# Turning the inverse transform's result by transposing DMAs within SBUF instead of on TensorE, for three of five channel groups

## The chip, the cores and the metric

The kernel runs on one core of one Trainium2 chip. The metric is the device time of one execution in microseconds (us), lower being better. The time before is the median of seven executions; a profile of one execution shows what each engine did in it.

## What is computed

The reference has two independent halves whose results are joined along the last axis. Half A is attention with a compressive memory, over four segments of 512 positions and 32 heads of 18 channels. Half B is a long convolution along the sequence, which the reference writes with Fourier transforms:

```python
# half A, for each segment s of 4 (L = 512, H = 32 heads, Dh = 18)
logits = einsum('bhqd,bhkd->bhqk', qs, ks) * scale + mask
a_dot  = einsum('bhqk,bhkd->bhqd', softmax(logits), vs)
a_mem  = einsum('bhld,bhde->bhle', phi(qs), M) / (einsum('bhld,bhd->bhl', phi(qs), z) + 1e-6)
o      = g * a_mem + (1 - g) * a_dot
M, z   = M + einsum('bhld,bhle->bhde', phi(ks), vs), z + sum(phi(ks))
a      = concat(o) @ wo                         # (2048, 576)
# half B (S = 2048 positions, D = 576 channels)
kv = shift4(k, shift_k) * v                     # a causal filter of 4 taps per channel
y  = irfft(rfft(pad(kv)) * rfft(pad(ssm_k)))[:S]
b  = q * (y + kv * ssm_D)
out = concatenate([a, b], axis=-1)              # (2048, 1152)
```

## The kernel before

All work is written down as some 1,360 pieces in a graph: each piece names the engines that may run it, what it reads and writes, and a priority. `schedule` deals the pieces to the five engines with a list scheduler that uses fixed durations, the priorities of the table `PRIO` (one integer for every piece, in the order in which pieces are created), the number of buffers of each kind (`SLOTS`) and the eight PSUM banks. It runs when the kernel is built; on the chip each engine then goes through its list in that order and waits on semaphores. So the table sets the order of everything, and a piece can be dealt to ACT or DVE, or to DVE or POOL, according to it. Almost all DMAs are issued from SP's queue, in list order; only the loads of `wq` and `wk` are issued from ACT.

Half A. For each segment, five transposing loads (L1032) bring x as `xT`; projections make queries and keys (`dn`), which go out to a scratch tensor in DRAM and come back per group of four heads as `pad` (L1073, three buffers). For each of the 32 head groups three score pieces on PE (L1293) are followed by exponentials on ACT (L1303, L1306), triangular masks on POOL (L1314) and the product with V on PE. The sums and results pass through DRAM scratch (`a_scratch`, `rs_scratch`) to be spread over partitions again as `cs`, `rs`, `rd` and `am`.

Half B. The channels are cut into five groups: four of 128 and one of 64. For each group:

- keys and values are loaded by transposing DMAs (L609, L612), filtered by matmuls with diagonal weights, multiplied and written to a scratch tensor; the filter `ssm_k` (kind h) and the product (kind x) are loaded as `xs`;
- `Dt`, a constant tensor made from `ssm_D`, is loaded once (L584) and added to the filter by `dadd` (L684) before its transform;
- two transform stages on PE (F1, F2) give spectra, which DVE and POOL multiply (`PQ`, L743 and L754);
- the inverse's first stage (`inv`) goes through PSUM and is copied to the tile `C` in four octants (`eC`). There is one buffer for `C`;
- **the turn**: `C` holds 128 partitions by 4096, which are 32 squares of 128x128 (16 in the last group). Eight at a time are transposed on PE against the identity into one PSUM bank (L802, the piece `ct`), and the bank is copied to a tile `CTp` of 128x1024 by ACT or DVE (the piece `ect`). There are three buffers for `CTp`;
- the inverse's last stage (`last`) multiplies the turned squares with the table `Psi`, DVE multiplies the result with q (L824, the piece `y`), and two DMAs store it (L831).

Groups 0 to 3 have four turns of eight squares each, group 4 has two: 18 turns in all.

The copies that the prediction names are those of helper `copy`: L365 on ACT, L367 on DVE. Matmuls go through `mm` (L359, and L361 for those placed in a part of the array). `zz` is a zeroed tile from which three DMAs (L985 and L992) fill the unused rows of the scratch tensor behind `pad`.

Of the kernel before, what the change touches and what calls it, by code (L numbers as in the profile page):

```python
# [12 lines left out]
ACT = mybir.ActivationFunctionType  # L13
# [5 lines left out]
P = 128  # L19
# [12 lines left out]
def c_act(n):  # L32
    return 0.06 + n * 0.00083
# [298 lines left out]
class Prog:  # L332
# [325 lines left out]
    def build_b(self):  # L658
        g, p = self.g, self.p
        for gi, (c0, Cg) in enumerate(GROUPS):  # L660
# [128 lines left out]
            for w in range(nc4 // 16):  # L789
                pl = Buf("ps2", "pslast")  # L790
                for v in range(2):
                    pt = Buf("ps1", "psct")
                    ct = Buf("CTp", "CTp")
                    vv = 2 * w + v
                    pr = tl + 2 * w + v

# [7 lines left out]
                    self.pe("ct%d.%d" % (gi, vv), 8 * 147, 8, tr, [Ct, self.ident], [pt], pr, al=[ct])  # L804
# [4 lines left out]
                    g.add("ect%d.%d" % (gi, vv), {"ACT": c_act(1024), "DVE": 0.075 + 1024 * 0.00052}, et, r=[pt], w=[ct], prio=pr)  # L809
# [671 lines left out]
    CV=[-35.266, 50.144, 61.906, 109.44, 129.026], flex=[-91.722, -31.756], lag_fin=193.527, pmode='d', qmode='f',  # L1481
)
# [17 lines left out]
-1149 -38 5 18 72 99 114 -74 -19 5 51 88 64 128 146 167 159 180 165 122 131 30 186 118 228 48 101 100 108 251 306 256  # L1500
263 352 380 245 253 21 331 182 192 229 -316 142 243 275 281 277 290 311 307 336 409 459 380 479 497 531 571 565 597
621 710 642 560 803 790 817 854 840 881 934 970 875 981 1058 1072 1085 1281 1268 1295 1346 1509 1296 1395 1491 1511
1525 1548 1538 1565 1582 109 63 10 89 -333 -29 95 64 60 224 310 27 229 284 281 119 208 60 236 249 29 54 253 109 83 255
-111 104 108 106 116 73 113 110 121 112 115 172 125 185 155 162 208 178 194 208 263 300 331 318 328 339 201 218 240
325 364 244 329 480 373 593 433 605 692 199 213 243 244 190 161 255 262 374 393 386 403 361 387 380 373 440 461 453
463 201 209 223 167 228 226 225 239 247 231 143 252 340 349 349 355 411 414 390 396 462 478 462 474 498 399 413 433
343 351 371 375 386 407 442 453 550 467 473 492 443 435 463 508 517 594 571 577 601 537 543 561 516 523 545 687 693
701 496 501 512 599 606 623 645 654 698 679 685 704 591 631 640 651 658 686 763 769 848 719 724 739 746 756 783 828
836 851 812 819 844 839 841 876 863 870 890 923 932 947 917 925 945 893 899 924 957 966 1044 764 804 922 1088 1114
1157 958 624 979 951 864 997 1237 939 1282 1198 1099 1251 1184 1155 1218 1331 1341 1350 1366 1321 1307 1322 1351 1469  # L1510
1462 1490 1525 1839 1832 1847 1860 341 352 376 486 498 560 575 593 631 656 671 723 708 743 735 751 819 869 882 890 608
696 757 856 927 871 819 965 1072 1174 1240 1355 1442 627 646 665 671 622 643 668 694 713 745 742 750 708 726 755 763
752 794 798 806 784 850 842 859 815 847 908 923 810 840 906 912 948 960 957 967 943 954 963 973 539 533 547 984 978
993 991 997 1006 972 964 981 1014 1028 1143 1178 1266 1245 1184 1253 1266 1295 1338 1354 1273 1321 1329 1359 1425 1376
695 699 770 778 836 838 930 938 1026 1030 1241 1255 1419 1068 1076 1094 1005 1012 1034 953 964 986 1105 1125 1148 1101
1107 1142 1163 1171 1182 1200 1210 1198 1183 1194 1218 1350 1357 1377 1133 1142 1164 1391 1408 1443 1237 1242 1269
1208 1214 1235 1292 1302 1339 1277 1339 1310 1326 1333 1352 1302 1309 1333 1367 1379 1386 1374 1383 1403 1398 1410
1430 1442 1456 1462 1428 1437 1457 1450 1461 1481 1475 1489 1509 1526 1537 1543 1534 1540 1562 1507 1513 1548 1576
1586 1591 1513 1544 1569 1630 1701 1741 1607 1258 1645 1654 1599 1838 1858 1904 1781 1852 1907 1892 1919 1871 1989
2004 1905 1864 1933 1946 2029 2021 2056 2053 2040 2046 2055 2077 2137 2143 2152 2164 2130 2123 2144 2157 1022 1029  # L1520
1049 1060 1075 1138 1114 1153 1180 1168 1185 1212 1187 1227 1378 1358 1401 1432 1413 1454 1167 1199 1280 1449 1517
1343 1539 1528 1696 1777 1829 1614 1915 1166 1177 1198 1203 1259 1291 1293 1298 1207 1216 1253 1258 1269 1312 1307
1321 1274 1287 1321 1335 1325 1348 1351 1360 1429 1466 1513 1524 1437 1469 1523 1537 1478 1488 1559 1572 1482 1498
1588 1598 1150 1157 1169 1621 1627 1636 1588 1613 1623 1602 1596 1611 1634 1652 1679 1734 1829 1834 1926 2006 2054
1944 2035 2046 2064 2108 2124 2057 2094 2099 1256 1265 1299 1306 1355 1371 1558 1562 1645 1650 1698 1713 2130 1560
1567 1586 1609 1616 1635 1584 1591 1609 1664 1679 1722 1693 1701 1722 1659 1666 1686 1736 1745 1752 1773 1779 1800
1719 1725 1743 1743 1750 1770 1817 1827 1839 1825 1832 1820 1800 1807 1796 1861 1870 1879 1905 1914 1907 1856 1863
1850 1881 1888 1877 1960 1970 1978 1932 1938 1923 1956 1962 1954 2004 2018 2024 2078 2087 2107 2016 2023 2011 2053
2061 2049 2115 2139 2146 2110 2116 2146 2155 2161 2181 2200 2210 2217 1934 2036 2072 2245 2267 2285 2100 1883 2135
2149 2107 2150 2195 2207 2352 2175 2395 2418 2302 2168 2340 2359 2316 2238 2365 2392 2471 2465 2479 2497 2496 2503  # L1530
2512 2521 2552 2558 2567 2581 2586 2592 2602 2621 1635 1663 1684 1700 1640 1805 1789 1817 1748 1777 1789 1868 1890
1927 1909 1921 1932 2082 2097 2108 1832 1805 1896 1947 2123 1959 2082 2312 2177 2380 2493 2435 2617 2046 2060 2066
2080 1861 1868 1873 1877 2105 2121 2159 2164 2012 2021 2063 2037 2134 2146 2162 2176 1760 1766 1775 2212 2220 2226
2247 2236 2254 2254 2261 2269 2188 2210 2229 2250 2304 2307 2427 2532 2538 2370 2389 2421 2258 2312 2325 2399 2434
2439 1618 1624 1618 1657 2376 2382 2410 2208 2215 2235 2182 2189 2224 2422 2432 2439 2243 2249 2269 2299 2309 2326
2357 2376 2383 2430 2437 2456 2352 2358 2417 2400 2409 2434 2478 2488 2501 2486 2492 2515 2454 2464 2502 2454 2464
2476 2510 2516 2537 2535 2542 2562 2599 2605 2627 2658 2668 2681 2570 2576 2603 2628 2634 2654 2672 2722 2693 2654
2661 2696 2833 2843 2932 2725 2730 2755 2877 2892 2919 2948 2961 2987 2974 2759 2768 2788 2696 2707 2727 2805 2815
2857 2899 2912 2861 2886 2567 2585 2611 2704 2724 2745 2640 2485 2685 2695 2656 2604 2691 2698 2769 2722 2812 2829
2779 2729 2816 2832 2970 2986 2978 2987 2995 3007 3085 3094 3076 3093 3098 3106 3068 3083 3046 3065 3087 3096 3025  # L1540
3039 3017 3038 3046 3050 250 346 388 470 365 381 382 406 362 373 511 610 620 619 631 590 599 604 609 417 425 668 692
686 699 713 897 911 428 431 698 849 708 858 871 943 954 432 440 935 1028 942 1035 1047 1091 1103 774 783 1036 1038
1042 1044 1063 1082 1093 92 186 1225 1233 1486 1230 1239 1480 1501 1260 1279 1648 1521 1530 1654 1667 1727 1746 515
606 816 830 779 793 908 918 785 804 779 1049 1049 1043 1048 1054 1060 1407 1408 1009 1016 1566 1679 1577 1687 1700
1945 1958 1456 1471 1711 1724 1716 1736 1749 1992 2003 1685 1692 1981 1987 1993 1994 1975 2065 2077 1886 1894 2150
2159 2165 2179 2196 2227 2236 1791 1798 2288 2294 2346 2294 2300 2333 2354 2316 2324 2381 2365 2369 2388 2394 2412
2418 773 869 1969 1977 1894 2010 1936 1945 1976 1983 1093 2278 2285 2283 2294 2177 2184 2272 2280 2001 2008 2308 2323
2313 2333 2344 2514 2526 2060 2069 2328 2340 2333 2348 2370 2412 2426 2267 2275 2438 2459 2445 2467 2480 2575 2594
2371 2375 2540 2559 2548 2566 2577 2603 2616 2457 2463 2632 2641 2685 2639 2648 2691 2702 2649 2657 2730 2720 2727
2736 2748 2765 2772 1457 1557 2490 2498 2445 2454 2614 2701 2393 2400 1982 2564 2572 2679 2688 2666 2674 2623 2630  # L1550
2644 2652 2701 2742 2713 2750 2761 2786 2797 2713 2720 2755 2768 2770 2781 2794 2819 2836 2750 2759 2795 2813 2802
2825 2834 2890 2906 2781 2788 2828 2847 2836 2862 2873 2900 2915 2845 2832 2926 2938 2948 2937 2956 2993 3001 2942
2965 2995 2954 2974 2999 3013 3033 3026 2290 2331 2800 2812 2840 2848 2626 2860 2872 2866 2875 2870 2883 2909 2914
2925 2925 2932 2961 2983 2884 2897 2921 2932 2936 2947 2957 3006 3022 1564 1557 2993 3040 3054 3041 3048 3060 3068
3082 3088
"""


def plan(prm=PRM, slots=SLOTS):
    pr = Prog(prm)  # L1560
    pr.build()
    if PRIO:
# [61 lines left out]
```

## Time and profile before

| | |
|---|---|
| median of 7 executions | 328.21 us (328.01 to 333.07) |
| the profiled execution | 330.75 us |
| its span in the profile | 329.0 us |
| mean granted TensorE clock | 0.964 of full speed |
| PE, DVE, ACT, POOL busy | 278.8, 254.0, 254.4, 154.8 us |
| DMA, SP's queue | 113,280 packets, 48.08 MB |

The span runs from the first to the last instruction on the core; the execution's own time is longer by what lies around it. PE is TensorE's matmuls, PEld its weight loads, DVE is VectorE, ACT is ScalarE, POOL is GpSimd, and SP is SyncE, whose row in a timeline (SPq) shows the time that its queue spends on issuing each DMA. A group's line ends with the idle time of the engine just before those instructions, and with what ended that idle time. The chain of work is followed back from the last instruction to what released it, step by step.

### The profile page before, as it was taken

The numbers are of one execution on the slowest core, as the hardware profiler recorded it, in microseconds if no ns is written. First come the engines' busy times: TensorE is split into PE (matmuls) and PEld (weight loads), VectorE is DVE, ScalarE is ACT, GpSimd is POOL, SyncE is SP. The second block draws the span as 40 slices with busy tenths as digits, with TensorE's granted clock in tenths as the row PEclk, the third lists the DMA queues.
The fourth block names the chain that finished last, engine by engine and source line by source line (L and its number), as shares of the span: only waits on it lengthen the run. The fifth ranks groups of instructions, "written<-read, shape, count | busy, mean of one in ns | idle before, by whom it ended". The sixth has DMA issues, their size and how long they took to land.

```text
span 329.0 us, 9734 instructions
## 1 busy us (share of the span) xinstructions
PE 278.8 (85%) x4073; PEld 190.6 (58%) x4083; DVE 254.0 (77%) x383; ACT 254.4 (77%) x251; POOL 154.8 (47%) x192
## 2 busy tenths in 40 slices
PE   1799779879898899898997998798987999886993
PEld 1656456455556665545565555555775576775882
DVE  6765666689797866867979558958899878998973
ACT  2465458798979889999977688879888889895940
POOL 8602032438546523855755237736738554325500
PEclk9999957999999999999999799989999999997998
DMA  8956898979998786499465795823343945143025
GB/s 183 304 91 203 164 175 204 146 222 196 154 183 182 178 140 187 156 262 210 141 147 116 141 251 191 175 95 116 103 122 91 189 143 133 59 89 64 4 57 114
DMA packets 114540, 50.03 MB, mean 152 GB/s; under 512 B 92206, under 2 KB 107328, under 8 KB 114496
## 3 DMA queue, kind: packets, MB, share of 16 engines
q1 hardware_dynamic: 113280, 48.08, 64.7%
q10 hardware_dynamic: 1216, 1.33, 1.6%
q8 instruction: 32, 0.52, 0.7%
q14 instruction: 12, 0.10, 0.1%
HBM read 25.31 MB, written 16.87 MB: 128 GB/s over the span
## 4 chain that ended last, share of the span: by engine, by line
PE 37%; ACT 21%; DVE 16%; DMA 12%; issue 7%; SPq 4%; POOL 1%; ACTq 0%; DVEq 0%; POOLq 0%
PE PS L359 24%; ACT P L1303 11%; PE PS L361 7%; DMA wq<-in_A_wq_dram 5%; PE PS L1293 4%; ACT P L1306 3%; DMA rs<-rs_scratch 3%; DVE PQ L743 2%; DMA Dt<-in_B_ssm_D_dram 2%; SPq L992 2%; DVE C L367 1%; DVE Hx L367 1%; DVE dn L367 1%; DMA qk_scratch<-dn 1%; ACT PQ L365 1%
## 5 line engine op out<-in xcount | busy, mean ns | idle before, releaser
L1314 POOL TENSOR_SCALAR_AFFINE_SELECT P<-P 128x512 bf16<-128x512 bf16 (+1 forms) x112 | 81.6, 741 | 107.7 <-ACT P L1303 70.8
L1303 ACT ACTIVATE P<-PS 128x2048 bf16<-128x2048 f32 x54 | 101.6, 1881 | 14.3 <-PE PS L1293 12.4
L1306 ACT ACTIVATE P<-PS 128x1024 bf16<-128x1024 f32 x52 | 50.6, 1031 | 6.3 <-PE PS L1293 6.3
L1293 PE MATMUL PS<-pad 25*128 25x384 bf16 (+3 forms) x512 | 35.1, 306 | 7.7 <-ACT P L1303 5.6
L359 PE MATMUL PS<-A,Ft 128*128 128x128 bf16 (+1 forms) x480 | 33.7, 220 | 7.6 <-DVE PQ L743 3.1
L359 PEld LDWEIGHTS <-Ft 128*128 128x128 bf16 x480 | 28.3, 101 | 13.0 <-issue 11.6
L361 PE MATMUL PS<-W,xs 128*64 128x128 bf16 x576 | 23.7, 235 | 8.3 <-DVE xs L684 3.6
L754 POOL TENSOR_TENSOR PQ<-PQ,Hx 128x1024 bf16<-128x1024 bf16 x11 | 23.4, 2123 | 13.4 <-ACT PQ L365 11.2
L361 PEld LDWEIGHTS <-xs 128*64 128x64 bf16 x576 | 20.2, 119 | 12.8 <-issue 7.7
L359 PE MATMUL PS<-xT,wq 128*126 128x512 bf16 (+1 forms) x100 | 26.0, 396 | 1.2 <-DMA wq<-in_A_wq_dram 0.8
L1293 PEld LDWEIGHTS <-pad 25*128 25x128 bf16 x512 | 11.8, 92 | 25.2 <-issue 21.1
L359 PE MATMUL PS<-xT,wk 128*126 128x512 bf16 (+1 forms) x100 | 25.1, 383 | 0.4 <-DVE C L367 0.4
L367 DVE CAST dn<-PS 126x1024 bf16<-126x1024 f32 (+1 forms) x15 | 18.3, 1221 | 9.0 <-PE PS L359 8.7
L361 PE MATMUL PS<-P,V 128*32 128x256 bf16 (+3 forms) x512 | 23.5, 302 | 2.0 <-DVE PQ L743 0.7
L359 PE MATMUL PS<-wo,am 126*128 126x288 bf16 (+1 forms) x144 | 22.5, 299 | 2.3 <-DVE Hx L367 1.8
L367 DVE CAST A<-PS 128x1024 bf16<-128x1024 f32 x18 | 21.8, 1220 | 3.4 <-PE PS L361 3.2
L359 PE MATMUL PS<-wv,xT 128*128 128x288 bf16 x160 | 22.4, 291 | 0.6 <-ACT dn L365 0.3
L1110 POOL TENSOR_TENSOR fk<-fk,dn 126x512 bf16<-126x512 bf16 (+1 forms) x10 | 11.6, 1156 | 23.2 <-DVE dn L1103 16.7
L365 ACT CAST A<-PS 128x1024 bf16<-128x1024 f32 x18 | 18.0, 1019 | 5.5 <-PE PS L361 5.0
L743 DVE TENSOR_TENSOR PQ<-PS,Hx 128x1024 bf16<-128x1024 f32 x18 | 21.7, 1212 | 0.3 <-PE PS L359 0.2
L361 PEld LDWEIGHTS <-V 128*32 128x32 bf16 x512 | 11.4, 96 | 15.4 <-issue 4.3
L359 PEld LDWEIGHTS <-xT 128*128 128x128 bf16 x160 | 15.7, 100 | 7.0 <-issue 2.3
(148 smaller groups left out, 576.9 us busy)
## 6 DMA issues: line engine op xcount, KB each, us to landing
pad<-qk_scratch SPq DMA_DIRECT2D x32, 256.0 KB
qk_scratch<-dn SPq DMA_DIRECT2D x16, 252.0 KB
a_scratch<-ou SPq DMA_DIRECT2D x30, 128.0 KB
out_dram<-oA SPq DMA_DIRECT2D x16, 144.0 KB
q<-in_B_q_dram SPq DMA_DIRECT2D x8, 256.0 KB
xs<-in_B_ssm_k_dram SPq DMA_DIRECT2D x4, 512.0 KB
kv_scratch<-X SPq DMA_DIRECT2D x4, 512.0 KB
xs<-kv_scratch SPq DMA_DIRECT2D x4, 512.0 KB
```

What stands on the lines that cost most here:

```text
L359: self.nc.tensor.matmul(out, lhsT=lhsT, rhs=rhs, start=start, stop=stop)
L361: self.nc.tensor.matmul(out, lhsT=lhsT, rhs=rhs, start=start, stop=stop, tile_position=pos)
L365: self.nc.scalar.copy(out=out, in_=in_)
L367: self.nc.vector.tensor_copy(out=out, in_=in_)
L743: self.nc.vector.tensor_tensor(out=self.t(T)[:], in0=self.psf(pp), in1=self.t(H)[:], op=ALU.mult)
L754: eng.tensor_tensor(out=self.t(T)[:], in0=self.t(T)[:], in1=self.t(H)[:], op=ALU.mult)
L992: e.dma_start(out=dst, in_=self.t(zz)[0:96, 0:1792])
L1110: eng.tensor_tensor(out=v, in0=v, in1=self.t(dense[m])[0:M, w_, :], op=ALU.add)
L1293: nc.tensor.matmul(o, lhsT=t[r, 1, q0:q0 + P], rhs=t[r, 0, q0:L], start=True, stop=True, tile_position=(32 * j, 0))
L1303: self.nc.scalar.activation(out=d[:], in_=self.PS[:, a:a + 4, :].rearrange("p a f -> p (a f)"), func=ACT.Exp, scale=scale)
L1306: self.nc.scalar.activation(out=d[:, 1024 * k:1024 * k + 1024], in_=self.PS[:, x:x + 2, :].rearrange("p a f -> p (a f)"), func=ACT.Exp, sc ...
L1314: self.nc.gpsimd.affine_select(out=ap, in_=ap, compare_op=ALU.is_ge, fill=0.0, base=0, pattern=pat + [[1, P]], channel_multiplier=-1)
```

## The change

For groups 0, 1 and 2 the eight PE transposes of each turn and the copy out of PSUM are taken out, and one DMA on SP's queue takes their place: it reads 128x1024 of `C` and writes the eight transposed squares to `CTp`. Groups 3 and 4 keep PE and the copy. The graph gets 12 pieces fewer on balance (24 out, 12 in). The DMA reads the whole of `C`'s group as far as waiting goes: it waits for all four octants, as the PE transposes did. Priorities of all pieces are replaced by a new table, so that the order on each engine, and which of two engines gets a copy or product, differ throughout.

```diff
             for w in range(nc4 // 16):
                 pl = Buf("ps2", "pslast")
                 for v in range(2):
-                    pt = Buf("ps1", "psct")
                     ct = Buf("CTp", "CTp")
                     vv = 2 * w + v
                     pr = tl + 2 * w + v
+                    if p["ctm"][gi] == "d":
+                        def td(e, vv=vv, Ct=Ct, ct=ct):
+                            e.dma_start_transpose(out=self.t(ct)[:].rearrange("p (i c) -> p i c", i=8), in_=self.t(Ct)[:, 1024 * vv:1024 * vv + 1024])
+
+                        self.dma("ctd%d.%d" % (gi, vv), td, [Ct], [ct], pr - 3, P * 2048, pk=256, kind="t", issue=1.4)
+                    pt = Buf("ps1", "psct") if p["ctm"][gi] == "p" else None
...
-                    self.pe("ct%d.%d" % (gi, vv), 8 * 147, 8, tr, [Ct, self.ident], [pt], pr, al=[ct])
+                    if pt:
+                        self.pe("ct%d.%d" % (gi, vv), 8 * 147, 8, tr, [Ct, self.ident], [pt], pr, al=[ct])
...
-                    g.add("ect%d.%d" % (gi, vv), {"ACT": c_act(1024), "DVE": 0.075 + 1024 * 0.00052}, et, r=[pt], w=[ct], prio=pr)
+                    if pt:
+                        g.add("ect%d.%d" % (gi, vv), {"ACT": c_act(1024), "DVE": 0.075 + 1024 * 0.00052}, et, r=[pt], w=[ct], prio=pr)
...
+    ctm='dddpp', ndir=0,
...
 PRIO = """
...
```

The function `dma` puts the piece on SP's queue; its figures `issue`, `pk` and `kind` are used by the scheduler alone.

## The prediction

> **What bounds the kernel now.** I began with the page's first two parts: how busy each engine is, and where in the span.
>
> ```profile
> PE 278.8 (85%) x4073; PEld 190.6 (58%) x4083; DVE 254.0 (77%) x383; ACT 254.4 (77%) x251; POOL 154.8 (47%) x192
> ...
> PE   1799779879898899898997998798987999886993
> ...
> DMA  8956898979998786499465795823343945143025
> ```
>
> TensorE (PE) is the busiest engine, and from the third slice on it stands at 8 or 9 tenths in most slices. DMA is nearly full in the first third and half idle after some 200 us. No engine is full for the whole span, so the next view is the chain that ended last:
>
> ```profile
> PE 37%; ACT 21%; DVE 16%; DMA 12%; issue 7%; SPq 4%; POOL 1%; ACTq 0%; DVEq 0%; POOLq 0%
> ```
>
> The end is set by a relay between PE, ACT and DVE. An instruction taken off one of them pays in full only where it is a link of the chain, but none of the three has much slack to hide it in. Then the groups that the change touches, among the groups by form:
>
> ```profile
> L802 PE MATMUL PS<-ident,C 128*128 128x128 bf16 x144 | 10.3, 219 | 1.3 <-ACT P L1303 0.7 <-DVE ou L367 0.3 <-DVE nm L1185 0.3
> ...
> L367 DVE COPY CTp<-PS 128x1024 bf16<-128x1024 bf16 x11 | 7.3, 684 | 1.7 <-PE PS L802 1.5
> L365 ACT COPY CTp<-PS 128x1024 bf16<-128x1024 bf16 x7 | 6.9, 1026 | 0.7 <-PE PS L802 0.7
> ```
>
> That is 144 transposes in 18 blocks of eight, and 18 copies; groups 0 to 2 have 12 blocks and 12 copies of them. Last, the chain in order of time, where these and two front pieces stand:
>
> ```profile
> 29.33 6.05 SPq L992
> 36.03 0.60 SPq L1073
> 36.72 6.13 DMA Dt<-in_B_ssm_D_dram
> 43.23 1.92 PE PS L361 x32
> ...
> 129.95 0.62 PE PS L802 x8
> 130.59 0.81 ACT CTp L365
> ...
> 133.44 0.61 PE PS L802 x8
> ...
> 160.84 0.64 ACT CTp L365
> ...
> 241.20 0.69 DVE CTp L367
> ...
> 250.14 0.68 DVE CTp L367
> ...
> 284.10 0.61 PE PS L802 x8
> ```
>
> **Removed.** In the timeline the 12 blocks of groups 0 to 2 stand as runs of 1.05, 0.61, 0.61, then 1.07, 0.61, 0.62, then 1.05, 0.61, 0.61 us: 6.84 us of PE. Asking the copies by window gives 3 on ACT (3 x 1.03 = 3.1 us) and 9 on DVE (9 x 0.68 = 6.1 us). What lay on the chain is the last seven pieces above: 0.62 + 0.81 + 0.61 + 0.64 + 0.69 + 0.68 + 0.61 = **4.7 us**. The bounds: nothing, if another engine's work fills every gap; 6.8 us, if PE alone were the limit. Even then something is late next: in the stretch 132 to 165 us, ACT is busy 31.6 of 33 us, so there a shorter PE only lets ACT's exponentials queue. I take the 4.7 that the chain shows.
>
> **Added.** Twelve transposing DMAs on SP's queue, each turning 128x1024 within SBUF: 1024 rows of 256 bytes. No row shows one with its source in SBUF. The nearest rows are the loads that turn from DRAM, by their lines:
>
> ```profile
> L1032 SPq DMA_TRANSPOSE xT<-in_A_x_dram x15: 1122/1211/3142, 40.6 to 181.1; - x15
> ...
> L612 SPq DMA_TRANSPOSE X<-in_B_v_dram x5: 2202/2662/6580, 10.1 to 137.7; - x5
> ```
>
> Those are min/median/max ns of queue time for 512 rows and for 2048 rows. 1024 rows lie between: 1.5 us, or 12 x 1.5 = 18 us of SP. Here the Trainium skill speaks against the change. "VectorE: DVE Perf Modes", section "The three transpose paths", gives 390 ns for a 128x128 square on TensorE and 1309 ns through the DMA crossbar, and its table of rules sends such squares to TensorE where PSUM will do. By the page the 96 squares would take 37 us off PE and put 126 us, or 10.5 per DMA, on the DMA side: a clear loss. The trace differs on both: eight squares take 0.61 us of PE, and the four squares of an xT load hold the queue for 1.21 us. I take the trace's 1.5 us and keep the page's 10.5 as the far end.
>
> Where this falls: in the changed queue of 259 entries group 0's four stand at 91, 95, 98 and 107, group 1's at 168, 169, 178 and 185, group 2's at 221, 222, 225 and 236. What stood there before (the earlier turns deducted) ran at about 126 to 141, 202 to 226 and 264 to 285 us. Adding SP's rows of the timeline, SP is busy 25.0 of 33 us from 132 on and 12.1 of the 15.4 us from 126 to 141.4, but only 17.5 to 19.7 of 33 from 198 to 297. So groups 1 and 2 fit into idle time. Group 0's 6 us meet 3.3 us of it; 2.7 us become delay for what is queued behind: scores' `pad` loads, `rs` and `rd` broadcasts, `dn` stores. `pad` has three buffers, so loads run ahead of the scores that read them; most of the 2.7 is covered. If that cover is gone, all 6 us count. On the engines, a packet takes 64.7% x 16 x 329 / 113280 = 30 ns:
>
> ```profile
> q1 hardware_dynamic: 113280, 48.08, 64.7%
> ```
>
> 1024 packets over 16 engines are 1.9 us of all sixteen per DMA, 23 us in all, against 21 to 25% free between 99 and 165 us and about half free later. I take **1 us** for SP and DMA together, between 0 and 6.
>
> A new wait: SP waits for the last copy into C before each group's first turn, and the group's last matmuls wait for the landing. A small transfer shows 2.6 us from issue to landing on the chain (`cs` at 236.06), so a turn lands some 4 us after issue, where block plus copy took 1.3 to 1.6. For group 0 this is covered: C is complete at 119 and turned only at 130. Group 2 has no such lead (C complete at 275.0, first transpose at 275.5), but the changed PE order puts 28 other pieces of work between `inv2.2` and `last2.0`, and C is not needed again before group 3's inverse. In the end phase groups 3 and 4 stay on PE, so the tail is as before. I add nothing.
>
> **Moved.** Every piece of work has a new priority, so all five orders differ. Two things can be read from the orders. First, how work is dealt out: counting each kind by its row's mean, ACT loses 3.0 us in all, DVE 4.3 and POOL 2.3, so nothing is overloaded in exchange. Second, the load of `Dt`: before, it was SP's 24th entry, behind the zero fill at L992 whose issue took 6.05 us, and DVE and then PE waited 3.7 and 3.6 us for it. Now it is the 13th, ahead of that fill. PE's 3.6 us idle before 43.23 goes; late next are the `pad` and `dn` transfers behind the fill, and in the windows view DMA is 98% busy from 33 to 66 us, so not all of it comes through. Bounds 0 and 3.6; I take **2 us**. For the rest of the reordering no row gives a size. The windows view by tenths has PE idle for 2.4 to 5.7 us in each of the eight inner ones; taking 1.7 as the swing of each, 1.7 x root 8 gives about 5 us either way, my estimate of what a new order can do by itself; its middle is zero.
>
> **Sum.** -4.7 + 1 - 2 = -5.7 us, against the profiled execution's 330.75 (span 329.0 and 1.75 around it): 325.0. The median of the runs shown is 328.21, 2.5 lower, and the same step gives **322.5**, 1.7% less.
>
> **Rivals.**
> *Refilled.* PE's and DVE's freed time is taken by waits for ACT, whose 152 us of exponentials (101.6 + 50.6) do not change, and the `Dt` gain by full DMA engines. For it: ACT's 31.6 of 33 us at 132 to 165, and 21% of the chain on ACT. Against it: seven links of the chain are removed work. Time: -1 + 1 = 0, so 328.
>
> *Clogged queue, slower.* The turn within SBUF holds SP for far longer than a load that turns. Place: group 0, where 3.3 us are idle. Two `pad` buffers ahead, at one head group per 329/32 = 10 us, give perhaps 10 us of lead; so it decides from (10 + 3.3)/4, about 3.3 us per DMA. At 6 us group 0 is 4 x (6 - 3.3) = 11 us late, and groups 1 and 2 (24 us each, against 10 to 11 idle and 10 of lead) 3 to 4 us each: 18 in all, less the 6.7 gained, is +11, or 339.5. At 5 us it is 7 for group 0 and, by estimate, 2 to 3 each for turns that land late under the other two: 12 - 6.7 = +5, or 333.5. For it: no row shows such a source, and the page's price lies beyond the point. Against it: 2048 rows from DRAM, twice as many, take 2.7.
>
> *The new order, not the turn.* The swing of 5 us above decides, with either sign, and the DMAs are neutral. This is taken into the ranges of the others.
>
> **How the numbers follow.** The forecast gets 0.58, the refill 0.20, the clogged queue 0.22. The likeliest one's own range is 322.5 with the swing of 5 and a little for the bounds: 316.5 to 328. To hold 8 in 10 the range goes down to 315 (6.8 on the chain, 3.6 at the front, and the larger part of the swing) and up to 334, into the slower case at 5 us per DMA. A measurement of this kernel tells about 1% (3.3 us) from no change. Faster by more than that: 0.57, nearly the forecast's share; within 1%: 0.21; slower: 0.22.
>
> **What would show it.** Right: 12 `DMA_TRANSPOSE` of CTp at 1.2 to 2 us of SP each; `L802`'s successor with 48 transposes instead of 144; PE near 272 us busy, DVE near 250; no wait for `Dt` near 40 us; SP's delay at 126 to 145 not followed by a scores' wait for `pad`. Wrong: turns of over 3.3 us in SP's queue, last-stage matmuls waiting for CTp by DMA, PE idle growing by as much as its work shrank, or, at the front, another transfer in `Dt`'s place.

## The result, and the profile after

The kernel after the change takes 327.03 us (median of 27 runs, 322.75 to 329.78); before, taken beside it, 329.65 us (64 runs). The ratio is 0.9904, with a 95% interval of 0.9882 to 0.9926: a gain of 1.0%, or 3.2 us of 329.65 by the ratio and 2.6 by the medians, where 5.7 were forecast. Runs of one kernel differ by one or two per cent, so ratios and their intervals are used below; disturbed runs are left out of them.

The page of the execution profiled after the change (span 326.5 us, mean granted clock 0.977), in the rows that were shown of before:

```profile
PE 271.0 (83%) x3978; PEld 184.1 (56%) x3987; DVE 252.2 (77%) x378; ACT 251.3 (77%) x233; POOL 150.1 (46%) x189
...
PE   0699977879889898799888869899898598777994
...
DMA  8989997987999587998996858689566573554025
...
q1 hardware_dynamic: 125952, 51.22, 74.8%
...
PE 38%; ACT 21%; DVE 18%; DMA 11%; issue 7%; SPq 2%; POOL 0%; DVEq 0%; ACTq 0%
```

PE and ACT lost about the work that was foreseen: PE has 7.8 us less to do (278.8 to 271.0) and ACT 3.1; DVE has only 1.8 less, where 4.3 had been counted. But the span fell by 2.5 us. PE's idle time, span less busy, grew from 50.2 to 55.5 us: of the work that was taken off PE, more than half came back as waiting. In the tenths 15 slices stand at 9, where 19 did.

The turns and the load of `Dt`, each asked for by its line (duration in ns as min/median/max, then first and last start in us):

```profile
L807 PE MATMUL PS<-ident,C x48: 216/219/230, 303.5 to 316.8; 128*128 128x128 bf16 x48
```

```profile
L797 SPq DMA_TRANSPOSE CTp<-C x12: 1261/1326/4931, 125.8 to 279.7; - x12
```

```profile
L584 SPq DMA_DIRECT2D Dt<-in_B_ssm_D_dram x1: 828/828/828, 15.9 to 15.9; - x1
```

48 transposes are left on PE, a turn by DMA holds SP's queue for 1.33 us in the median (one of the twelve for 4.9; all together 20.7 us, where 18 had been estimated), and `Dt` is issued at 15.9 instead of 36.7 us. In the chain of after the place of `Dt` is taken by another small load, that of `beta`:

```profile
35.15 4.42 DMA bt<-in_A_beta_dram
```

### The profile page after: what moved, and what is told of

It reads as the page before. It is cut to its first block, busy times and chain, and to the rows that moved or that the text cites. A ratio compares the mean times of both kernels' runs of the same rounds, so it can differ in the third digit from the quotient of the medians.

```text
span 326.5 us, 9497 instructions
## 1 busy us (share of the span) xinstructions
PE 271.0 (83%) x3978; PEld 184.1 (56%) x3987; DVE 252.2 (77%) x378; ACT 251.3 (77%) x233; POOL 150.1 (46%) x189
## 3 DMA queue, kind: packets, MB, share of 16 engines
q1 hardware_dynamic: 125952, 51.22, 74.8%
q10 hardware_dynamic: 1216, 1.33, 1.4%
## 4 chain that ended last, share of the span: by engine, by line
PE 38%; ACT 21%; DVE 18%; DMA 11%; issue 7%; SPq 2%; POOL 0%; DVEq 0%; ACTq 0%
PE PS L359 26%; ACT P L1310 13%; PE PS L361 7%; PE PS L1300 4%; DMA rs<-rs_scratch 3%; DVE PQ L743 3%; DMA rs_scratch<-rb 2%; DMA qk_scratch<-dn 2%; DVE A L367 1%; DVE C L367 1%; DMA a_scratch<-ou 1%; DMA bt<-in_A_beta_dram 1%; ACT A L365 1%; DMA out_dram<-oA 1%; DVE PS L1378 1%
## 5 line engine op out<-in xcount | busy, mean ns | idle before, releaser
L1310 ACT ACTIVATE P<-PS 128x2048 bf16<-128x2048 f32 x68 | 128.0, 1882 | 26.1 <-PE PS L1300 25.7
L1321 POOL TENSOR_SCALAR_AFFINE_SELECT P<-P 128x512 bf16<-128x512 bf16 (+1 forms) x112 | 80.5, 731 | 103.3 <-ACT P L1310 82.2
L1300 PE MATMUL PS<-pad 25*128 25x512 bf16 (+3 forms) x512 | 34.5, 305 | 13.7 <-ACT P L1310 10.2
L754 POOL TENSOR_TENSOR PQ<-PQ,Hx 128x1024 bf16<-128x1024 bf16 x13 | 27.6, 2126 | 12.2 <-ACT PQ L365 10.6
L361 PE MATMUL PS<-W,xs 128*64 128x128 bf16 x576 | 23.0, 226 | 8.5 <-DVE X L642 2.0
L1313 ACT ACTIVATE P<-PS 128x1024 bf16<-128x1024 f32 x24 | 23.5, 1042 | 4.9 <-PE PS L1300 4.9
L361 PEld LDWEIGHTS <-xs 128*64 128x64 bf16 x576 | 19.0, 112 | 13.3 <-issue 11.8
L359 PE MATMUL PS<-wv,xT 128*128 128x288 bf16 x160 | 23.1, 291 | 1.1 <-DVE V L367 0.6
L359 PE MATMUL PS<-X,dg 128*128 128x512 bf16 x71 | 19.0, 381 | 1.6 <-ACT P L1310 0.8
L359 PE MATMUL PS<-PQ,GP 128*128 128x128 bf16 (+1 forms) x160 | 18.1, 214 | 2.3 <-ACT P L1310 1.1
```

Source lines behind the costliest of these rows:

```text
L359: self.nc.tensor.matmul(out, lhsT=lhsT, rhs=rhs, start=start, stop=stop)
L361: self.nc.tensor.matmul(out, lhsT=lhsT, rhs=rhs, start=start, stop=stop, tile_position=pos)
L754: eng.tensor_tensor(out=self.t(T)[:], in0=self.t(T)[:], in1=self.t(H)[:], op=ALU.mult)
L1300: nc.tensor.matmul(o, lhsT=t[r, 1, q0:q0 + P], rhs=t[r, 0, q0:L], start=True, stop=True, tile_position=(32 * j, 0))
L1310: self.nc.scalar.activation(out=d[:], in_=self.PS[:, a:a + 4, :].rearrange("p a f -> p (a f)"), func=ACT.Exp, scale=scale)
L1313: self.nc.scalar.activation(out=d[:, 1024 * k:1024 * k + 1024], in_=self.PS[:, x:x + 2, :].rearrange("p a f -> p (a f)"), func=ACT.Exp, sc ...
```

## The experiments

Names that begin with old_ keep the order of before, those with new_ the order of after. Each kernel's ratio is to before, run beside it. Line numbers shift by some 5 to 7 between the kernels: before's L1063 is L1068 or L1070.

### Dt's load alone, and the change without it

old_dt is before with one entry of the order moved; new_dtlate is after with that entry put back behind the fill and the loads of `beta`.

```diff
# old_dt, at the end of plan(); move(name, ahead) re-inserts a piece ahead of another
+    move("Dt", "sk")
# new_dtlate, the same place in after
+    move("Dt", "qd0.3")
```

> The kernel before, with one DMA moved: the load of Dt is issued as SP's 10th instead of 24th, ahead of the fill at L992; nothing else. It prices the front term by itself. The prediction's 2 us: 0.4 to 0.8% below before. Theory 6 (PE's wait for Dt is replaced by the next transfer that is late, DMA being full): within 0.2% of before.

> The changed kernel with one DMA moved back: Dt's load stands as SP's 24th again, behind the second fill (now L999), beta and a pad, as it stood before the change; all else as in the changed kernel. Moving it forward in the kernel before gave 0.9903 of before. Theory A (the Dt load is all of the change's gain, and turn with new order come out even): 0.997 to 1.003 of before. Theory B (the turn and the order have a gain of their own, since the front of the changed kernel is held by another transfer, beta's, anyway): at most 0.993 of before.

Measured: old_dt **0.9903** [0.9873, 0.9933], new_dtlate **1.0000** [0.9973, 1.0028]. So the moved load is worth 3.2 us (0.0097 x 330.2) by itself in the old order, and without it nothing is left of the change's gain: the twelve turns and the new order together come out at nothing, within 0.3%. PE's timeline shows what the move does: before, F1's first matmuls start at 43.23 after 3.58 us idle; in old_dt they start without a wait.

```profile
43.23 1.92 PE L361 MATMUL PS<-W,xs 128*64 128x128 bf16 x32 [3.58 <-DVE xs L684]
```

```profile
39.40 0.64 PE L361 MATMUL PS<-W,xs 128*64 128x128 bf16 x16
```

In new_dtlate the wait is back, here at the weight loads of F1's matmuls (a line of waits gives total, times and longest, in us):

```profile
PEld L361 <- DVE xs L684: 3.6, 1, 3.6
```

The difference between the starts of the same exponential in the traces of old_dt and before is nothing at 39 us, 4.4 us at 53, 5.1 at 156, and 3.1 at the end; some 1.5 us of it go between 254 and 259 us. These are two single executions; the ratio is the measure of the gain.

### Is it the wait, or the clock after it?

PE's granted clock falls after the idle stretch in before. old_fill gives PE something to do in it, and leaves `Dt` late.

```diff
                     def f1(...):
+                        if (gi, kind, u) == (0, "h", 3):
+                            for i in range(14):
+                                self.mm(o[:, 0, :], self.t(self.ident)[:], self.t(self.w["wq"])[:, 0, 0:512], True, True)
```

> Before with Dt's load where it was, and fourteen dummy matmuls of 512 columns on TensorE in the 3.6 us in which it waits for Dt; their results are overwritten. Theory that the idle stretch is what the granted clock answers to: PEclk in 44 to 56 us rises from 0.64 to near 1.0 and the time falls by 1 to 2 us, 0.993 to 0.997. Rival, that the clock there is set by something else: PEclk stays near 0.64 and the ratio is 1.000 or, where the dummies run past Dt's arrival, a little more.

> The same kernel as old_fill, run again: its granted clock in 44 to 56 us was 1.00 where before's was 0.64, and its ratio 1.0009 had an interval of 0.9% around it. Theory that the lost clock is a good part of what Dt's move gains: 0.994 to 0.997. Rival, that it is the wait itself and the work behind it, and that a faster TensorE in those 12 us only waits longer later: 0.999 to 1.002.

The windows from 44 to 52 us (PE, PEld, DVE, ACT and POOL busy with their counts, then the granted clock, the DMA share and GB/s), first before, then old_fill, and PE's timeline of old_fill at the end:

```profile
44.00:52.00 8.00, 7.98 (x98) 6.24 (x94) 5.92 (x11) 6.20 (x7) 2.90 (x3) 0.50 0.95 155
```

```profile
44.00:52.00 8.00, 5.67 (x95) 3.61 (x91) 6.71 (x13) 7.57 (x8) 3.38 (x4) 1.00 0.83 194
```

```profile
38.55 3.20 PE L359 MATMUL PS<-wq,ident 128*128 128x512 bf16 x13
41.67 1.08 PE L361 MATMUL PS<-W,xs 128*64 128x128 bf16 x32
```

Before runs those 8 us at half the clock: 98 matmuls keep PE busy for 7.98 us. With the dummies the clock is full and 95 matmuls take 5.67. This agrees with what the Trainium skill says in "TensorE: Matmul & The Clock Gate", section "Why this matters for your kernels": a gap of over some 3 us between matmuls drops the clock to half; here 3.58 us did, and the clock stood at 0.50 from 44 to 52 us. But the time does not follow: **1.0009** [0.9965, 1.0053], and **1.0003** [0.9960, 1.0046] in the second run, where 0.994 to 0.997 would have shown a part of the gain in the clock. Both runs together (1.0006, give or take 0.0031) leave the clock at most 0.8 us. So most of what `Dt`'s move gains is the wait, and the work behind it that starts earlier. That the lost clock fell on work which was not the last to be waited for is the likely reason; no trace here shows it.

### Is beta's load next?

old_dtbeta moves both small loads in the old order, new_beta moves `beta` ahead of `Dt` in the new one.

```diff
# old_dtbeta
+    move("Dt", "sk")
+    move("beta", "sk")
# new_beta
+    move("beta", "Dt")
```

> The kernel before with the loads of Dt and of beta both ahead of SP's 10th, nothing else; turns on PE. If the front pays whatever small load is freed from behind the fill: 0.985 to 0.989 of before (ACT waited 2.3 us for beta there). If beta's wait was covered by other work: as with Dt alone, 0.988 to 0.993.

> After, with the load of beta moved from behind the fill of qk_scratch to just ahead of Dt's load. In the profile of after that load lies on the chain that ended last, and ACT waits 1.7 us for it near 38 us. Theory that the front of the new order is still bound by a small load behind the fill: down by 1 to 1.7 us, 0.985 to 0.988 of before, under both kernels. Rival, that what ACT does there is soon waited for by nothing, as in before's order, where beta's move beside Dt's changed nothing (0.9904 against 0.9903): 0.990.

Measured: **0.9904** [0.9871, 0.9937] beside old_dt's 0.9903, and **0.9895** [0.9836, 0.9955] beside after's 0.9904. ACT's wait for `beta` (1.7 us in after) goes, and the time stays. The link of 4.42 us on the chain was worth nothing that can be measured, and no version here beats after by a measurable amount.

### What is the removed work worth in the old order?

old_dt_skip is old_dt without the turns and copies of groups 0 to 2. Its transposes and copies are gone and no DMA is added; POOL zeroes the three `CTp` tiles once, at 62 to 71 us, so that the last stage of these groups works on zeros.

```diff
                     def tr(...):
+                        if gi < 3:
+                            return
...
                     def et(...):
+                        if gi < 3:
+                            return
```

> The order of before with Dt's load early (the run of that alone stood at 0.990 of before), and the twelve turns of groups 0 to 2 left out altogether, TensorE's part and the copies: CTp holds zeros for these groups, so their share of the output is wrong. Theory of the prediction's sum (the removed work stood on the path, 4.7 us): 0.990 - 4.7/330 = 0.976. Theory that an order fitted to before fills nothing in, because other waits end at the same time: 0.987 to 0.990. If it is 0.976 here and was 0.987 in the new order without turns, the new order itself costs about 1%.

Measured: **0.9922** [0.9884, 0.9960]. That is no better than old_dt: 0.0019 above it, give or take 0.0048 (the two half-widths, 0.0030 and 0.0038, added as squares). The sum's 4.7 us would have been 0.9761; by the interval at most 1 us of it can be there. The zeroing does not hide a gain in the traces: the same exponential starts 0.6 us later than in old_dt at 48 us, before it, and 0.65 us later at 110, after it. The pages, old_dt first:

```profile
PE 277.3 (85%) x4073; PEld 189.1 (58%) x4083; DVE 253.8 (78%) x383; ACT 254.2 (78%) x251; POOL 154.2 (47%) x192
```

```profile
PE 270.3 (83%) x3978; PEld 183.4 (56%) x3987; DVE 249.7 (77%) x374; ACT 252.2 (78%) x248; POOL 156.7 (48%) x195
```

PE has 7.0 us less work, ACT 2.0, DVE 4.1, and the span went from 325.8 to 325.4. Where it went is seen in the chain in order of time, at the place where the prediction counted `CTp` copies at 241 and 250 us. First old_dt:

```profile
236.52 1.28 DVE CTp L367 x2
237.80 0.03 issue
237.83 0.70 DVE nm L1185
238.53 0.04 issue
238.57 0.62 PE PS L802 x8
239.19 0.02 issue
239.22 1.02 ACT CTp L365
240.24 0.03 issue
240.27 1.21 DVE PQ L743
...
245.52 0.68 DVE CTp L367
246.19 1.14 DVE Hx L367
```

Then old_dt_skip:

```profile
235.48 4.77 DMA xs<-in_B_ssm_k_dram
240.25 0.02 issue
240.28 0.04 DVE xs L684
240.31 0.06 issue
240.38 1.21 DVE PQ L743
...
243.83 2.32 DVE am L1426
246.15 1.15 DVE Hx L367
```

Four pieces with 2.9 us of removed work (two copies of 1.28 together, a turn of 0.62, a copy of 1.02) stood ahead of the product `PQ` at 240.27. Without them it starts at 240.38. DVE's own rows of old_dt_skip tell why; the brackets hold the idle time before each and what ended it:

```profile
237.01 0.69 DVE L1190 TENSOR_TENSOR nm<-PS,rd 126x512 bf16<-126x512 f32 x1 [0.91 <-ACT A L365]
...
240.28 0.23 DVE L684 TENSOR_TENSOR xs<-xs,Dt 128x16 bf16<-128x16 bf16 x1 [0.85 <-DMA xs<-in_B_ssm_k_dram]
```

The 1.3 us of copies that DVE no longer makes turn into 0.91 us of waiting for ACT, and what is left of the lead into 0.85 us of waiting for the load of group 4's filter, which lands at 240.25. In old_dt DVE came to that load at 240.16 and found it there. (Here the load took longer: it was issued 0.5 us earlier, at 235.48 against 235.98. How close behind it usually lies, two executions cannot tell.) The same again at 246: a copy is gone, and DVE's `am` ends at the same time. Earlier it is no different: where old_dt's chain has a turn at 128.47, that of old_dt_skip runs over the transfers of `pad` (128.63, 2.88 us) and `qk_scratch` (131.53, 3.87 us), and from 131 to 165 us, past group 0's turns, its exponentials stay 0.6 to 0.85 us behind those of old_dt. The links were on the path, but a second path lay close beside them.

### What do the DMAs cost in the new order?

new_skip and new_skip2 are after with the twelve DMAs left out. In the first POOL zeroes `CTp` at the start, in the second later, at some 50 to 65 us.

```diff
                         def td(...):
-                            e.dma_start_transpose(...)
+                            pass
```

> The changed kernel in its own order, but the twelve turns of groups 0 to 2 are not issued at all (CTp is zeroed once at the start, so the last stage of these groups works on zeros); everything else stays. It prices the DMAs as they stand: SP's time, the sixteen engines' time and the waits for landing. Theory 1 (the DMAs cost more than the 1 us of the prediction: group 0 falls where DMA is full): 3 to 5 us faster than the changed kernel, 1.9 to 2.4% below before. Theory 2 (the DMAs are nearly free, and it is the removed PE and copy work that is worth less than 4.7 us, or the front that gave nothing): within 1 us of the changed kernel, 0.8 to 1.3% below before.

> The changed kernel in its own order without the twelve turning DMAs, as new_skip, but the three CTp buffers are zeroed by POOL at about 50 to 65 us, where it has room, instead of at the start, where new_skip's first stretches came some 2 us late (the last stage of groups 0 to 2 works on zeros). If the DMAs are nearly free: 0.988 to 0.993 of before, as the changed kernel. If they cost more than the 1 us of the prediction: 0.985 or less.

new_skip gave **0.9985** [0.9957, 1.0013], slower than after, though it only leaves work out. Why I could not settle. In its one trace, of an execution that took 332.86 us, the first exponentials come 0.6 us late, but at 48 us they are level with those of after again; they fall 2.9 us behind near 120, where a load of `pad` ends a wait of the scores. That the zeroing causes this is not shown. new_skip2 differs from new_skip in nothing but the place of the zeroing and gave **0.9874** [0.9817, 0.9932]. The two stand 1.1% apart, so a difference of less than 1% between two kernels here is laid to an edit with care. After's 0.9904 is 0.0030 above new_skip2, give or take 0.0062: by this pair the DMAs cost some 1 us, and anything between nothing and 3 us is possible; new_skip does not fit it. Their packets can be priced in the same order by the DMA part of new_skip2's page:

```profile
q1 hardware_dynamic: 113280, 48.08, 66.7%
```

74.8% of 326.5 less 66.7% of 324.5 are 27.8 us of sixteen engines for 12 turns and 12,672 packets: 2.3 us a turn, 35 ns a packet. This is the difference of two executions, and includes whatever the turns' packets cost the others.

### The turn by DMA in the old order

old_dma takes the order of before, and in groups 0 to 2 the DMA replaces the turn as early as `C` and `CTp` allow.

```diff
                     def tr(...):
+                        if gi < 3:
+                            self.nc.sync.dma_start_transpose(out=<CTp, 8 squares>, in_=<1024 columns of C>)
+                            return
```

> The kernel before in its own order, every other piece left in its place; only the turns of groups 0 to 2 become DMAs, each issued as early as C and its CTp buffer allow, and their transposes and copies go. The turn alone, without the new order. Theory 1 (the turn carries the gain, the new order adds little): 0.6 to 1.4% below before. Theory 3 (the turn is neutral and the new order is what is measured): within 0.3% of before. Theory 4 (the turn needs a new order around it, since the last stage waits for the landing): 0.3% or more above before.

Measured: **1.0418** [1.0362, 1.0474], 342.63 us. SP's timeline and the waits of 119 to 140 us:

```profile
120.49 4.11 SPq L799 DMA_TRANSPOSE CTp<-C  x3
...
127.15 0.82 SPq L1068 DMA_DIRECT2D qk_scratch<-dn  x1
```

```profile
DVE dn L1108 <- DMA qk_scratch<-dn: 5.4, 2, 4.5
...
PE PS L359 <- DVE dn L367: 3.5, 1, 3.5
```

Three turns hold SP for 4.1 us, and behind them stands the store of the next block of q and k, which went out at 124.30 before. The buffer `dn` that it reads comes free late, DVE waits for it, and PE for DVE. That is the smaller part of the loss: the same exponentials as in before are 1.0 us early at 124 us, 3.3 late at 137, 7.0 late at 254 and 14.5 late at 289. In the last of these steps group 2's turns stand on the chain, ahead of a load of `rs`:

```profile
282.82 6.87 SPq L799 DMA_TRANSPOSE CTp<-C  x3
```

To see whether the place or the packets did that, two kernels turn group 0 alone by DMA, with `Dt` early: old_dt_g0 (run twice, the second as old_dt_g0b) one turn at a time where SP stood idle, old_dt_g0early the first three together ahead of that store.

```diff
# old_dt_g0 and old_dt_g0b
+    move("ct0.0", "rsb0.2"); move("ct0.1", "pad1.6"); move("ct0.2", "ad13"); move("ct0.3", "ad14")
# old_dt_g0early
+    move("ct0.0", "qd2.1"); move("ct0.1", "qd2.1"); move("ct0.2", "qd2.1"); move("ct0.3", "ad14")
```

> The order of before with Dt's load early, and only group 0's four turns by DMA, each placed singly where SP's queue stood idle in before (near 130, 142, 151 and 161 us). Theory that a turn costs by what is queued behind it: nothing is pushed, 0.990 or less, down to 0.990 - 2.7/330 = 0.982 if all of the removed TensorE work and copies of group 0 was on the path. Rival, that the transposing packets cost by themselves, by taking DMA engines and SBUF from others: the 3.2 us that group 0 lost in the order of before come back wherever they stand, 0.990 + 3.2/330 = 1.000.

> As the run before, but group 0's first three turns issued together at about 120 us, ahead of the store of the second q and k block. Theory that what is queued behind them costs: the store goes out some 3 us later, qk_scratch's readers with it, and the ratio is about 1.000 (0.990 + 3.2/330). Rival, that the packets cost by themselves: the same as the run with the turns apart, within 0.3%.

> The same kernel as old_dt_g0, run again, since six runs that lay between 323.5 and 331.7 us left an interval of 2% there. Theory that a turn in a stretch in which SP's queue is idle costs nothing and that the TensorE work which it removes is worth nothing either: 0.990, as Dt's move alone. Rival, that its packets delay the small gathers of rs and rd next to them (the profile of old_dt_g0 shows ACT waiting 2.6 us at 137 us behind that chain): 0.995 to 1.000, with the early run, 1.010, above it in both cases.

Measured: apart **0.9882** [0.9782, 0.9982] and **0.9941** [0.9905, 0.9976]; together **1.0099** [1.0047, 1.0150]. The same four DMAs cost 2.0% more than old_dt in one place (6.5 us, give or take 2) and 0.4% (1.3, give or take 1.5) in the other, by its second, closer measurement. The first three together cost about twice the 3.2 us that the theory had put. SP's store of `dn` and the waits of 119 to 145 us, first in old_dt:

```profile
123.56 0.84 SPq L1063 DMA_DIRECT2D qk_scratch<-dn  x1
```

```profile
DVE dn L1103 <- DMA qk_scratch<-dn: 2.3, 2, 1.2
```

Then in old_dt_g0early, with the turns ahead of the store:

```profile
123.03 4.47 SPq L799 DMA_TRANSPOSE CTp<-C  x3
127.61 0.85 SPq L1068 DMA_DIRECT2D qk_scratch<-dn  x1
```

```profile
DVE dn L1108 <- DMA qk_scratch<-dn: 5.1, 2, 3.8
...
ACT P L1311 <- PE PS L1298: 4.2, 2, 3.7
PE PS L1298 <- DVE nm L1190: 3.7, 1, 3.7
```

The store goes out 4 us later than in old_dt, at 127.61, DVE waits 5.1 us for it instead of 2.3, and PE and ACT wait behind DVE. So most of the cost is the place in the queue. In after, the planner puts the first three turns of group 0 singly behind those stores, and the fourth behind the load of a filter:

```profile
124.24 0.84 SPq L1070 DMA_DIRECT2D qk_scratch<-dn  x1
125.75 1.37 SPq L797 DMA_TRANSPOSE CTp<-C  x1
...
128.84 1.17 SPq L1070 DMA_DIRECT2D qk_scratch<-dn  x1
130.06 1.32 SPq L797 DMA_TRANSPOSE CTp<-C  x1
132.72 1.42 SPq L797 DMA_TRANSPOSE CTp<-C  x1
...
140.42 0.39 SPq L677 DMA_DIRECT2D xs<-in_B_ssm_k_dram  x1
140.91 4.93 SPq L797 DMA_TRANSPOSE CTp<-C  x1
```

### How far an order swings

old_jitter is before with its priorities shifted by a fixed pattern of up to 1 us; new_pe is after's table with the turns on PE, planned anew.

```diff
# old_jitter
-            o.prio = int(x) / 10.0
+            o.prio = int(x) / 10.0 + (o.i * 7919 % 21 - 10) / 10.0
# new_pe
-    ctm='dddpp', ndir=0,
+    ctm='ppppp', ndir=0,
```

> The kernel before with every priority shifted by a fixed amount between -1.0 and +1.0 us: the same work, the same instructions, turns on PE, Dt's load still 24th, but another order. It sizes what a new order does by itself, for which the prediction had put 5 us either way and a middle of zero. That estimate: within 1.5% of before, either sign. If the table before was fitted, so that any unfitted order loses: 1.5% to 4% above before, and then old_dma's and new_pe's losses are the price of an order that does not fit, not of the turn.

> The changed kernel's table of priorities, but with the turns of all groups on PE again (each transpose and copy has the priority that its DMA had). The new order alone, as near as the planner lets it be. Theory 1: within 0.4% of before. Theory 3: 0.6 to 1.2% below before, as the changed kernel. Theory 5 (the new order by itself is a loss, that the turn has to make up): 0.5% or more above before.

Measured: **1.0460** [1.0402, 1.0517] and **1.0316** [1.0261, 1.0371]. Priorities that are off by at most 1 us cost 4.6%, some 14 us by the medians. new_pe therefore can't tell what the turn is worth in the new order: by these two kernels, a table that was fitted to one set of pieces doesn't fit another.

## Why the prediction was right and wrong

**The sign was right, for a part of the reason.** Term by term, against the working on record:

| term | forecast | measured |
|---|---|---|
| removed work on the path | -4.7 us | none seen in the old order (old_dt_skip beside old_dt); by the interval not over 1 us |
| turns by DMA | +1 | about +1 in the new order (0 to 3, new_skip2); not settled, as new_skip does not fit |
| `Dt` | -2 | -3.2 |
| new order | 0, swing 5 | turns, removed work and order together 0.0, give or take 0.9 (new_dtlate) |

**The step that failed is the sum of the chain's seven pieces, 4.7 us.** The prediction named nothing as the lower end and then took the whole of it, as if every link of the chain paid in full. Left out in old_dt_skip, the same work gave 0.9922 beside old_dt's 0.9903, where the sum asked for 0.9761. Its rival *Refilled* named the mechanism, and it is what the runs show for the turn. What filled the gaps was wider than ACT's exponentials, though: a copy on ACT, a load that lands at the same time, and another instruction of DVE. The rival had `Dt`'s gain swallowed too, and there it was wrong. On the 328.21 us that the prediction started from, 0.9904 is 325.1: about as far from the rival's 328 as from the forecast's 322.5.

**The second term that was mis-sized is `Dt`**: 2 us taken from bounds of 0 and 3.6, measured 3.2, which is all of the gain. The reason for the discount, the `pad` and `dn` transfers behind the fill that would be late next, did not come in: in old_dt's trace the gain grows past 3.6 us, to 5.1, and part of it is lost only after 250 us. Its replacement on the chain, `beta`, was the named sign of a wrong forecast ("another transfer in `Dt`'s place"); old_dtbeta and new_beta show that it did no harm.

**The turn by DMA was priced well.** 1.5 us of queue for a turn, measured 1.33; 30 ns a packet, measured 35; so 2.3 instead of 1.9 us of sixteen engines. The price of 1309 ns for a square that the Trainium skill gives ("VectorE: DVE Perf Modes", section "The three transpose paths") did not carry over to a DMA of eight squares in a row: 27.8 us for 96 squares are 0.29 us a square. Nothing was put down for the new wait, and rightly: in after no engine waits for the landing of a turn (in old_dma PE does once, for 2.8 us). The clogged queue at 3.3 us a turn did not come; single turns passed that, and those over 4 us stand right behind a load of `xs`. No wait of scores for `pad` shows in after at 120 to 150 us, as forecast; but `pad` was the wrong thing to look at. What is tight behind those turns is the store of `dn`, which was named among what is queued and was already a link of 4.04 us in the chain of before at 124.30. The new order keeps group 0's turns behind it; the old order with early turns did not, and paid.

**The swing of the order was neither sized nor centred right.** It was put at 5 us either way around zero. Both orders that were not fitted to their pieces cost 3 to 5%, some 9 and 14 us by the medians, and none gained. The two fitted tables differ by little: without any turns the old order stands at 0.9922 and the new one at 0.9874, whose intervals overlap.

What stays open: whether the new order itself gains up to 1 us that the DMAs then cost, or neither does anything; the intervals do not tell. Whether a turn placed singly in the old order costs 1 us or nothing is open too.

## What to carry to other kernels

A link of the chain that ended last is worth only its lead over the second path into the same place: before adding up removed links, look at each point where the chain rejoins, and ask what else ends there within the time that is taken out. In an in-order queue a new DMA costs what stands behind it, so find the entry behind it that is already on the chain, and put it after that one. When a change moves everything, run its smallest moved piece alone: here one load moved ahead of a long fill was the whole gain.

## What the runs showed of the hardware

- A transposing DMA within SBUF of 128x1024 (2 bytes an element) holds SP's queue for 1.26 to 1.4 us as a rule, about as long as one of 512x128 from DRAM (1.21), and takes some 2.3 us of sixteen DMA engines.
- The longest holds of SP's queue by turns go with one place: in the traces each turn of over 4 us stands right behind a load of `xs`, of 512 or 256 KB (4.93 us in after at 140.91, 4.71 in old_dt_g0b at 149.12, 4.10 in old_dma at 282.82). Other entries in that place were held as well: the zero fill for 6.05 us in before at 29.33, a store of `dn` for 6.36 in after at 27.50, a load of `pad` for 4.71 in before at 87.74. It is not always so: in old_dt a load of `rs` at 237.30 was held for 0.77. No run moved such an entry away, so the cause is not shown.
- After 3.58 us without a matmul the granted clock was 0.50 from 44 to 52 us; with the gap filled it stayed at 1.00. The time of the kernel was the same either way, within 0.4%, which I had not expected of a clock that is halved on the busiest engine.
